# Four attention layers in one kernel: values ahead of background work, and VectorE's softmax chain in memory of its own and in more parts of the final layer

## The chip, the cores and the metric

The kernel runs on one core of a Trainium2 chip. The metric is the device time of one execution in microseconds (us). The engines of the core are TensorE (PE), VectorE (DVE), ScalarE (ACT), GpSimd (POOL) and SyncE (SP, which issues DMAs here). Each works off its own list of instructions in order and waits on semaphores.

## The reference

Four layers act on x of 2048 rows by 640, in bf16, each with 32 heads of 20 columns. Layers 0 and 2 use weights A and a causal window of 256 keys; layers 1 and 3 use weights B and attend to all 2048 keys.

```python
def _A_ref(x, wqkv, wo):          # _B_ref: the same without the mask
    qkv = (x @ wqkv).reshape(B, S, 3, H, Dh).transpose(2, 0, 3, 1, 4)
    q, k, v = qkv[0], qkv[1], qkv[2]
    scores = einsum("bhqd,bhkd->bhqk", q, k) * (Dh ** -0.5)
    mask = (idx[:, None] - idx[None, :] >= 0) & (idx[:, None] - idx[None, :] < 256)
    p = softmax(where(mask, scores, -1e9))
    return einsum("bhqk,bhkd->bhqd", p, v).transpose(0, 2, 1, 3).reshape(B, S, D) @ wo
x = A_x
x = x + _A_ref(_layernorm(x), A_wqkv, A_wo)
x = x + _B_ref(_layernorm(x), B_wqkv, B_wo)
x = x + _A_ref(_layernorm(x), A_wqkv, A_wo)
x = x + _B_ref(_layernorm(x), B_wqkv, B_wo)
```

## The kernel before, in words

**Units, banks and tiles.** The queries are cut into four chunks `c` of 512, the heads into eight groups `g` of four. A *unit* is one layer, chunk and group (`Unit`, L674). A unit's work is a list of *banks*: the scores of 128 keys against 512 queries for one head `j`, which fill one PSUM bank of 128x512 float32. A full unit has 16 key blocks times 4 heads, so 64 banks. The first chunk of layers 1 and 3 is cut into *parts* by key blocks (`PARTS`, L42): layer 1 into four parts of 4 blocks, layer 3 into one of 12 blocks (48 banks) and one of 4. Results of a part that isn't the last are kept in `raw_o`.

**A tile** is what one pass of the main loop (from L1281) handles: three banks, sometimes two or four. PSUM has eight banks: 0 to 2 for the scores of even tiles, 3 to 5 for odd ones (a tile of four takes bank 6 too), 7 for the values' sums (`op`), and bank 6 for everything else. A loop pass, called a tick below, writes instructions in this order:
- the tile's scores on TensorE (L1318), "S" below; if VectorE is to take a bank of it, the first step of that bank's chain follows;
- one exponential on ScalarE over the tile's banks (L1349), into a buffer `pt`;
- `load_ahead`, which issues DMAs of coming units, then `pump` and `keep_clock`: **background work** (projections, layer norm, output products, the tails that divide by the softmax sums), in slices of some 0.2 us of TensorE, by a credit that `rate` (L1258) sets from what is due; `keep_clock` adds matmuls whose results nobody reads (`unread`, L639) where there is too little. All of it goes through bank 6, and each product there must be moved out by VectorE (L323, L568, L1092 and others) before the next may start;
- **the values** (L1382): the probabilities of the tile two or three passes back times v, added up in bank 7; at a unit's end the banks that VectorE computed are multiplied too (L1391), and `finish_unit` (L841) has VectorE copy bank 7 out (L848, L850, L862, L864);
- one step of VectorE's chain (`side_step`, L953), and the masks of windowed tiles on GpSimd and VectorE (L1421, L1431).

The built order of each engine is the order of these calls; nothing reorders it.

**VectorE's chain.** A unit's `aside` (L684) names banks whose exponential VectorE computes, in pairs: two conversions of scores to fixed point (L920, one for each bank), then over both banks L925, L931, L936, L944 and L948. `t_side` (L897) yields after each; a step may be taken when `side["credit"]` is above zero; the credit grows by 0.4 a tick and, once `side_start` (L876) has set `late`, by 1.2 or 1.1. Two kinds of place are used:
- layer 1, chunks 1 to 3: two banks of each unit. Such a bank is the third bank of a tile of two others ("side" in the list made up to L1233), so that the exponential of that tile covers two banks. The chain's three buffers and two outputs lie in `raw_o`, which is free in that time.
- layer 3 from chunk 1 on (after the list, `t >= len(tiles)`): six banks of nearly every unit, whose scores are computed alone into bank 6 (L914). The three buffers are taken from the pool of normalized inputs `xnT` once all of those are free, the outputs from `ka` and `qa`.

The first chunk of layer 3 has no such banks. `xnT` has five buffers (L72), the keys of windowed units 18 (`KA`, L38).

Of the kernel before, what the change touches and what calls it, by code (L numbers as in the profile page):

```python
# [9 lines left out]
BF16 = mybir.dt.bfloat16  # L10
# [27 lines left out]
KA = 18  # L38
SIDE_RATE = 1.2
QA = 4  # L40

# [7 lines left out]
def kernel(  # L49
# [14 lines left out]
    def pool(name, bufs, space=None):  # L64
        kw = {"space": space} if space else {}
        return ctx.enter_context(tc.tile_pool(name=name, bufs=bufs, **kw))
# [4 lines left out]
    vap = pool("vap", 10)  # L71
    xtp = pool("xtp", 5)  # L72
    onp = pool("onp", 2)
# [28 lines left out]
    ka_all = big.tile([P, KA, C], BF16, name="ka", tag="ka")  # L102
    kas = [ka_all[:, n, :] for n in range(KA)]
    qa_all = big.tile([P, QA, C], BF16, name="qa", tag="qa")
# [197 lines left out]
    live = Counter()  # L302
    cap = {"qa": QA, "ka": KA, "va": 10, "xnT": 5, "kt": 3, "vt": 3, "qt": 4, "ln": 1, "w": 4, "vs": 2}

# [369 lines left out]
    class Unit:  # L674
        def __init__(self, l, c, g, part=None):
            self.l, self.c, self.g, self.part = l, c, g, part
            self.windowed = l % 2 == 0
            self.aside = ()
            if self.windowed:
                sets = [(m, b0, subs, j) for m, b0, subs in window_banks(c) for j in range(4)]  # L680
            else:

                if c > 0 and (l, c, g) != (3, 1, 0):
                    self.aside = tuple((NT - 1, j) for j in ((2, 3) if l == 1 else range(4)))  # L684
                    if l == 3 and (c, g) != (NC - 1, G - 1):
                        self.aside += ((NT - 2, 0), (NT - 2, 1))
                k0, k1 = key_blocks(l, part)
                sets = [
                    (None, 0, [(kc, 0, 4, 0)], j) for kc in range(k0, k1) for j in range(4)
                    if (kc, j) not in self.aside  # L690
                ]
            n = len(sets)
            self.banks = [
                (self, j, m, b0, subs, i < 4, i >= n - 4 + len(self.aside), i == n - 1)
                for i, (m, b0, subs, j) in enumerate(sets)
            ]
# [176 lines left out]
    side_out = {}  # L873
    side = {"credit": 0.0, "gen": None, "tiles": None, "late": False}

    def side_start():  # L876

        assert live["xnT"] == 0
        tl = [xtp.tile([P, KD, C], BF16, name="xnT", tag="xnT") for _ in range(3)]
        live["xnT"] += 3  # L880
        f = [v[:, 0:4, :].rearrange("p a b -> p (a b)") for v in tl[0:3]]
        side["tiles"] = [v.bitcast(F32) for v in f]
        side["out"] = deque(ka_all[:, KA - 6 + 2 * n : KA - 4 + 2 * n, :] for n in range(3))
        side["out"].extend(qa_all[:, 2 * n : 2 * n + 2, :] for n in range(2))
        side["late"] = True

    def side_early():

        b = part_o["t"]
        side["tiles"] = [b[:, 2 * n : 2 * n + 2, :].rearrange("p a b -> p (a b)") for n in range(3)]  # L890
        side["out"] = deque(
            b[:, n, :].bitcast(BF16).rearrange("p (a b) -> p a b", a=2) for n in (6, 7)
        )
        side["gen"] = t_side()
        side_step(False)

    def t_side():  # L897

        V = nc.vector
        while aside:  # L900
            u = aside[0]
            for pair in range(len(u.aside) // 2):
                while id(u) not in loaded or (
                    u.l == 3 and (not side["late"] or state["tick"] < loaded[id(u)] + 8)
                ):
                    yield None
                for i in range(2):
                    yield "bank"
                    xi, xm, xw = side["tiles"]
                    if u.l == 3:  # L910
                        mseq[0] += 1
# [17 lines left out]
                yield 0.7  # L929
                power = xw.bitcast(I16)[:, 0 : 2 * C]  # L930
                V.tensor_scalar(  # L931
# [50 lines left out]
    def side_need(u):  # L982

        if u.l == 3:
            n = 0
# [217 lines left out]
    with tc.manual_schedule():  # L1203
# [17 lines left out]
        while n < last_layer:  # L1221
# [4 lines left out]
            if (  # L1226
                len(at) < len(u.aside) and banks[n + 1][0] is u
                and len(tiles) >= 3 * len(at) + (at or [0])[0]
            ):
# [28 lines left out]
        def rate(t):  # L1258
# [11 lines left out]
            return min(1.1 * r, 1.0 if u.l == 0 else 0.9)  # L1270

        last_tick[0] = len(tiles)
        wide_pt = 0
# [7 lines left out]
        while ended is None or t < ended + 8:  # L1281
# [3 lines left out]
            if t < len(tiles) or banks:  # L1285
                if t >= len(tiles) and not side["late"] and not live["xnT"] and not todo:
                    side_start()
# [66 lines left out]
                for i, b in enumerate(cur):  # L1354
                    pts.append((t, pt, i, b))
                state["least"] = (1.76 if state["unit"] >= woven else 1.0) * n_b / 3
                state["floor"] = 0.9 if state["unit"] >= index[1, 1, 0, None] else 0.0
                load_ahead()
                r = rate(t)
                pump(r, r + 0.1)  # L1360
                keep_clock()
            else:
# [3 lines left out]
            for n in range(2 if n_b == 0 or t > closed + 1 else 0):  # L1366
# [30 lines left out]
                if end:  # L1397
# [3 lines left out]
                    break  # L1401

            if n_b:
                side["credit"] = min(side["credit"] + ((SIDE_RATE if state["unit"] < index[3, NC - 1, 0, None] else 1.1) if side["late"] else 0.4), 1.3)
                side_step(False)
# [73 lines left out]
```

## Time and profile before

| | |
|---|---|
| median of 3 runs (lowest to highest) | 2222.56 us (2214.69 to 2223.66) |
| the profiled execution's own time | 2214.42 us |
| its span on the core | 2212.7 us |
| exponentials L1349 on ScalarE | 2104.3 us in 1657 |
| PE, DVE, ACT, POOL busy | 1919.8, 1199.8, 2139.9, 482.5 us |
| two bank counts of L1349: 1536 columns (three banks), 1024 (two) | x1380, x198 |

Where the stages lie in the span, from the starts of L1349 taken tile by tile: layer 0, with the first parts of layer 1 woven in, up to 372 us; the rest of layer 1's first chunk to 492; chunks 1 to 3 of layer 1 with chunks 0 to 2 of layer 2 to 1293.7; the 12-block parts of layer 3 for groups 0 to 3 to 1382.1; chunk 3 of layer 2 to 1424.8; the 12-block parts of groups 4 to 7 to 1512.2; the 4-block parts to 1569.8; chunks 1 to 3 of layer 3 to 2202.0.

Busy times are sums of durations; where one instruction starts before the one ahead of it has ended, durations add up to more than the time that passes, so a price for a stream of them is read from the distance between starts. Idle times in the lines are those just before an instruction, with what ended them.

### The profile page before, as it was taken

The numbers are of one execution on the slowest core, as the hardware profiler recorded it, in microseconds if no ns is written. First come the engines' busy times: TensorE is split into PE (matmuls) and PEld (weight loads), VectorE is DVE, ScalarE is ACT, GpSimd is POOL, SyncE is SP. The second block draws the span as 40 slices with busy tenths as digits, with TensorE's granted clock in tenths as the row PEclk, the third lists the DMA queues.
The fourth block names the chain that finished last, engine by engine and source line by source line (L and its number), as shares of the span: only waits on it lengthen the run. The fifth ranks groups of instructions, "written<-read, shape, count | busy, mean of one in ns | idle before, by whom it ended". The sixth has DMA issues, their size and how long they took to land.

```text
span 2212.7 us, 70085 instructions
## 1 busy us (share of the span) xinstructions
PE 1919.8 (87%) x30415; PEld 756.1 (34%) x30415; DVE 1199.8 (54%) x2190; ACT 2139.9 (97%) x1734; POOL 482.5 (22%) x950
## 2 busy tenths in 40 slices
PE   8889998988888888888888888888888888888888
PEld 4444443333333333333333433342332222222222
DVE  6656564434445454444554533532467767767774
ACT  7889899999999999999999999999999999999998
POOL 6664545200231114301143112511000000000000
PEclk9999999999999999999999999999999999999999
DMA  6233323421211223112230123122121111111100
GB/s 200 74 99 91 88 81 93 102 78 45 74 41 33 71 60 97 33 34 66 66 104 24 48 72 100 36 57 63 54 62 35 32 32 44 32 32 35 49 24 16
DMA packets 88404, 137.09 MB, mean 62 GB/s; under 512 B 20766, under 2 KB 63486, under 8 KB 88094
## 3 DMA queue, kind: packets, MB, share of 16 engines
q1 hardware_dynamic: 68878, 79.43, 13.0%
q0 software_dynamic: 19216, 53.17, 8.1%
q8 instruction: 238, 3.90, 0.7%
q14 instruction: 72, 0.59, 0.1%
HBM read 99.52 MB, written 27.79 MB: 58 GB/s over the span
## 4 chain that ended last, share of the span: by engine, by line
ACT 52%; PE 21%; issue 18%; DVE 6%; DMA 1%; POOL 1%; ACTq 0%; DVEq 0%; POOLq 0%
ACT pt L1349 51%; PE ps L300 12%; PE ps L1318 5%; PE ps L1382 2%; DVE on L1092 1%; DVE st L323 1%; DVE pt L1431 1%; DMA wqk<-in_B_wqkv_dram 1%; PE ps L1088 1%; PE ps L437 0%; DVE on L864 0%; DVE x_sb L568 0%; DVE raw_o L920 0%; POOL pt L1421 0%; DVE xnT L323 0%
## 5 line engine op out<-in xcount | busy, mean ns | idle before, releaser
L1349 ACT ACTIVATE pt<-ps 128x1536 bf16<-128x1536 f32 (+2 forms) x1657 | 2104.3, 1456 | 41.8 <-PE ps L1318 32.1
L1318 PE MATMUL ps<-qt,kt 32*128 32x512 bf16 x3960 | 544.6, 384 | 91.4 <-ACT pt L1349 82.9
L300 PE MATMUL ps<-masks,ident 128*32 128x512 bf16 x5844 | 510.2, 387 | 117.8 <-ACT pt L1349 68.5
L1382 PE MATMUL ps<-pt,vt 128*21 128x512 bf16 x3908 | 397.6, 383 | 1.9 <-issue 1.0
L1318 PEld LDWEIGHTS <-kt 32*128 32x128 bf16 x3960 | 163.4, 91 | 546.4 <-issue 531.0
L300 PEld LDWEIGHTS <-ident 128*32 128x32 bf16 x5844 | 165.3, 94 | 349.9 <-issue 336.7
L1421 POOL TENSOR_SCALAR_AFFINE_SELECT pt<-pt 128x256 bf16<-128x256 bf16 (+2 forms) x505 | 213.8, 445 | 189.0 <-ACT pt L1349 183.5
L300 PE MATMUL ps<-xnT,wqk 128*32 128x512 bf16 x3320 | 224.6, 383 | 15.7 <-DVE st L323 4.0
L323 DVE CAST st<-ps 128x512 bf16<-128x512 f32 x134 | 92.7, 692 | 234.0 <-PE ps L300 230.4
L920 DVE TENSOR_SCALAR xnT<-ps 128x512 int32<-128x512 f32 x136 | 93.6, 688 | 134.1 <-PE ps L914 124.6
L300 PE MATMUL ps<-wop,on 128*32 128x320 bf16 x3712 | 159.8, 301 | 7.1 <-DVE x_sb L568 4.0
L1431 DVE TENSOR_TENSOR pt<-pt,masks 128x512 bf16<-128x512 bf16 (+4 forms) x267 | 112.4, 436 | 96.8 <-ACT pt L1349 94.6
L1382 PEld LDWEIGHTS <-vt 128*21 128x21 bf16 x3912 | 104.8, 91 | 126.1 <-issue 94.1
L300 PEld LDWEIGHTS <-on 128*32 128x32 bf16 x5760 | 113.5, 95 | 74.2 <-issue 51.1
L1318 PE MATMUL ps<-qa,ka 32*128 32x384 bf16 (+2 forms) x1408 | 114.7, 275 | 27.5 <-ACT pt L1349 24.4
L568 DVE TENSOR_TENSOR x_sb<-x_sb,ps 128x320 bf16<-128x320 bf16 x120 | 58.3, 486 | 146.8 <-PE ps L300 146.6
L300 PE MATMUL ps<-wv,xnT 128*32 128x320 bf16 x2560 | 115.2, 301 | 8.3 <-DVE on L1092 2.2
L1092 DVE TENSOR_TENSOR on<-on,ps 128x512 bf16<-128x512 bf16 x128 | 86.3, 684 | 57.9 <-PE ps L1088 56.7
L300 PEld LDWEIGHTS <-wqk 128*32 128x32 bf16 x3320 | 77.1, 95 | 114.4 <-issue 61.9
L864 DVE CAST on<-ps 128x512 bf16<-128x512 f32 x112 | 77.0, 687 | 57.0 <-PE ps L1391 32.6
L536 POOL DMA_DIRECT2D k_d<-st x75 | 43.0, 573 | 233.2 <-DVE st L323 223.2
L404 POOL TENSOR_SCALAR rstd<-mv 128x4 f32<-128x4 f32 x15 | 3.7, 248 | 382.6 <-DVE mv L391 374.4
(100 smaller groups left out, 1537.5 us busy)
## 6 DMA issues: line engine op xcount, KB each, us to landing
vt<-v_d SPq DMA_DIRECT2D x48, 336.0 KB
kt<-k_d SPq DMA_DIRECT2D x192, 80.0 KB
wqk<-in_B_wqkv_dram POOLq DMA_DIRECT2D x80, 160.0 KB, 3.4
wqk<-in_A_wqkv_dram POOLq DMA_DIRECT2D x70, 160.0 KB, 3.6
k_d<-st POOLq DMA_DIRECT2D x75, 128.0 KB, 2.6
q_d<-st POOLq DMA_DIRECT2D x75, 128.0 KB, 2.2
qt<-q_d SPq DMA_DIRECT2D x384, 20.0 KB
v_d<-vs POOLq DMA_DIRECT2D x16, 336.0 KB, 3.0
```

Source lines behind the costliest of these rows:

```text
L300: nc.tensor.matmul(out_[r], lhsT=lhsT[:, r], rhs=rhs, start=start, stop=stop)
L323: nc.vector.tensor_copy(out=out_, in_=in_)
L536: nc.gpsimd.dma_start(out=dst, in_=staging.pop())
L568: nc.vector.tensor_tensor(out=xv, in0=had, in1=yp, op=ALU.add)
L864: nc.vector.tensor_copy(out=oT, in_=op)
L920: V.tensor_scalar(out=xi.bitcast(I32)[:, i * C : (i + 1) * C], in0=side["psum"], scalar1=SCALE * LOG2E * FIX, scalar2=-127.0 * FIX, op0=AL ...
L1092: nc.vector.tensor_tensor(out=oT, in0=oT, in1=zb, op=ALU.mult)
L1318: nc.tensor.matmul(sp[:, i, col * P : (col + qn) * P], lhsT=u.k(kc, j), rhs=u.q(j, q0, qn), start=True, stop=True,)
L1349: nc.scalar.activation(out=pt[:, i:k, b0 * P :], in_=sp[:, i:k, b0 * P :], func=ACT.Exp, scale=SCALE,)
L1382: nc.tensor.matmul(op[32 * j : 32 * j + VW, q0 * P : (q0 + qn) * P], lhsT=u.v(kc, j), rhs=pg[:, i, col * P : (col + qn) * P], start=(first ...
L1421: nc.gpsimd.affine_select(out=v, in_=v, compare_op=ALU.is_gt if later else ALU.is_ge, fill=0.0, base=0, pattern=[[0, k - i], [-1 if later ...
L1431: nc.vector.tensor_tensor(out=pt_[:, i:k, cols], in0=pt_[:, i:k, cols], in1=mv_, op=ALU.mult)
```

## The change

1. Once `state["early"]` is off (from the first part of layer 1 with blocks 12 to 16, tile 307, 434 us), a tick's background work is written after the values instead of ahead of them.
2. The chain gets a tile `side_mem` (10 KB a partition) for its three buffers, and four 512-column blocks of `ka` as two outputs from the start. For this `xnT` goes from five buffers to three, and windowed keys from 18 blocks to 14.
3. Each 12-block part of layer 3's first chunk (eight units) names four banks, those of its last key block, for the chain. They are placed like those of layer 1: third bank of a tile whose exponential covers two, at tiles 0, 3, 8 and 11 of the part (`SIDE_AT`). The credit there grows by 0.9 a tick. (In layer 1 the two banks stay at 0 and 3.)
4. `side_start` no longer waits for `xnT` to be free.

```diff
+SIDE_AT = (0, 3, 8, 11)
-    xtp = pool("xtp", 5)
+    xtp = pool("xtp", 3)
-    kas = [ka_all[:, n, :] for n in range(KA)]
+    kas = [ka_all[:, n, :] for n in range(KA - 4)]
+    side_mem = big.tile([P, 10 * C], BF16, name="side", tag="side")
-    cap = {"qa": QA, "ka": KA, "va": 10, "xnT": 5, ...
+    cap = {"qa": QA, "ka": KA - 4, "va": 10, "xnT": 3, ...
 # Unit.__init__
-                if c > 0 and (l, c, g) != (3, 1, 0):
+                if l == 3 and c == 0 and part[0] == 0:
+                    self.aside = tuple((part[1] - 1, j) for j in range(4))
+                elif c > 0 and (l, c, g) != (3, 1, 0):
 # the chain's memory
-    side = {"credit": 0.0, "gen": None, "tiles": None, "late": False}
+    side = {
+        "credit": 0.0, "gen": None, "late": False,
+        "tiles": [
+            side_mem[:, 0 : 4 * C].bitcast(F32), side_mem[:, 4 * C : 8 * C].bitcast(F32),
+            side_mem[:, 8 * C : 10 * C],
+        ],
+        "out": deque(ka_all[:, KA - 4 + 2 * n : KA - 2 + 2 * n, :] for n in range(2)),
+    }
 # side_start
-        assert live["xnT"] == 0
-        tl = [xtp.tile([P, KD, C], BF16, name="xnT", tag="xnT") for _ in range(3)]
...
-        side["out"] = deque(ka_all[:, KA - 6 + 2 * n : KA - 4 + 2 * n, :] for n in range(3))
+        side["out"].append(ka_all[:, KA - 6 : KA - 4, :])
 # t_side, side_need
-                    u.l == 3 and (not side["late"] or state["tick"] < loaded[id(u)] + 8)
+                    u.l == 3 and u.c and (not side["late"] or state["tick"] < loaded[id(u)] + 8)
-                    if u.l == 3:
+                    if u.l == 3 and u.c:
 # the list of tiles
-                and len(tiles) >= 3 * len(at) + (at or [0])[0]
+                and len(tiles) >= SIDE_AT[len(at)] + (at or [0])[0]
 # main loop
+        def background(t, n_b):
+
+            state["least"] = (1.76 if state["unit"] >= woven else 1.0) * n_b / 3
+            state["floor"] = 0.9 if state["unit"] >= index[1, 1, 0, None] else 0.0
+            r = rate(t)
+            pump(r, r + 0.1)
+            keep_clock()
...
                 load_ahead()
-                r = rate(t)
-                pump(r, r + 0.1)
-                keep_clock()
+                if state["early"]:
+                    background(t, n_b)
...
 # (the values of this tick stand here)
+            if n_b and not state["early"]:
+                background(t, n_b)
             if n_b:
-                ... + ((SIDE_RATE if ... else 1.1) if side["late"] else 0.4), 1.3)
+                ... + ((SIDE_RATE if ... else 1.1) if side["late"] else 0.9 if units[state["unit"]].l == 3 else 0.4), 1.3)
                 side_step(False)
```

More of the change, by code (lines that the diff above doesn't have):

```diff
@@ L302 @@
     live = Counter()
-    cap = {"qa": QA, "ka": KA, "va": 10, "xnT": 5, "kt": 3, "vt": 3, "qt": 4, "ln": 1, "w": 4, "vs": 2}
+    cap = {"qa": QA, "ka": KA - 4, "va": 10, "xnT": 3, "kt": 3, "vt": 3, "qt": 4, "ln": 1, "w": 4, "vs": 2}
     def room(*tags):
@@ L873 @@
     side_out = {}
-    side = {"credit": 0.0, "gen": None, "tiles": None, "late": False}
-    def side_start():
-        assert live["xnT"] == 0
-        tl = [xtp.tile([P, KD, C], BF16, name="xnT", tag="xnT") for _ in range(3)]
-        live["xnT"] += 3
-        f = [v[:, 0:4, :].rearrange("p a b -> p (a b)") for v in tl[0:3]]
-        side["tiles"] = [v.bitcast(F32) for v in f]
-        side["out"] = deque(ka_all[:, KA - 6 + 2 * n : KA - 4 + 2 * n, :] for n in range(3))
+    side = {
[6 more added lines that the diff above has]
+    }
+    def side_start():
+        side["out"].append(ka_all[:, KA - 6 : KA - 4, :])
         side["out"].extend(qa_all[:, 2 * n : 2 * n + 2, :] for n in range(2))
@@ L887, in side_early @@
     def side_early():
[L889 to L893, printed above, removed]
         side["gen"] = t_side()
@@ L929, in t_side @@
                 yield 0.7
-                power = xw.bitcast(I16)[:, 0 : 2 * C]
+                power = xw.bitcast(I16)
                 V.tensor_scalar(
@@ L982, in side_need @@
     def side_need(u):
-        if u.l == 3:
+        if u.l == 3 and u.c:
             n = 0
@@ L1285 @@
             if t < len(tiles) or banks:
-                if t >= len(tiles) and not side["late"] and not live["xnT"] and not todo:
+                if t >= len(tiles) and not side["late"] and not todo:
                     side_start()
@@ L1355 @@
                     pts.append((t, pt, i, b))
-                state["least"] = (1.76 if state["unit"] >= woven else 1.0) * n_b / 3
-                state["floor"] = 0.9 if state["unit"] >= index[1, 1, 0, None] else 0.0
                 load_ahead()
-                r = rate(t)
-                pump(r, r + 0.1)
-                keep_clock()
+                if state["early"]:
+                    background(t, n_b)
             else:
@@ L1401 @@
                     break
+            if n_b and not state["early"]:
+                background(t, n_b)
             if n_b:
-                side["credit"] = min(side["credit"] + ((SIDE_RATE if state["unit"] < index[3, NC - 1, 0, None] else 1.1) if side["late"] else 0.4), 1.3)
+                side["credit"] = min(side["credit"] + ((SIDE_RATE if state["unit"] < index[3, NC - 1, 0, None] else 1.1) if side["late"] else 0.9 if units[state["unit"]].l == 3 else 0.4), 1.3)
                 side_step(False)
```

## The prediction, made before the changed kernel ran

> **What bounds the kernel now.** I read the busy times first, then the costliest groups, then the waits.
>
> ```profile
> PE 1919.8 (87%) x30415; PEld 756.1 (34%) x30415; DVE 1199.8 (54%) x2190; ACT 2139.9 (97%) x1734; POOL 482.5 (22%) x950
> ...
> L1349 ACT ACTIVATE pt<-ps 128x1536 bf16<-128x1536 f32 (+2 forms) x1657 | 2104.3, 1456 | 41.8 <-PE ps L1318 32.1
> ```
>
> ScalarE's exponentials fill the span; 41.8 us of idle stand ahead of them, mostly because the scores (S) came late. So time can be won in two ways: fewer banks for ScalarE, or S on time. The waits say why S comes late: TensorE stands in background work until VectorE has emptied bank 6.
>
> ```profile
> PE ps L300 <- DVE st L323: 22.6, 75, 0.6
> ...
> PE ps L300 <- DVE on L1092: 15.1, 31, 1.7
> ```
>
> (Total, times, longest.) The next view is the timeline, without which neither edit has a price.
>
> ```profile
> 888.96 0.39 PE L1382 MATMUL ps<-pt,va 128*21 128x384 bf16 x8
> ...
> 891.00 0.68 DVE L1092 TENSOR_TENSOR on<-on,ps 128x512 bf16<-128x512 bf16 x1
> ...
> 891.72 0.40 PE L300 MATMUL ps<-masks,ident 128*32 128x512 bf16 x4 [0.85 <-DVE on L1092]
> ...
> 892.38 0.40 PE L1382 MATMUL ps<-pt,vt 128*21 128x512 bf16 x4
> ```
>
> At 890.87 TensorE begins to wait 0.85 us in background work, and the values at 892.38, whose inputs are long there, stand behind it and ahead of the next S. Four column groups run at once: four values products cost the next instruction some 0.22 us.
>
> ScalarE's own pace I take from the distances between starts of L1349: behind a three-bank tile 1.331 us where nothing waits, behind a two-bank tile 0.904 at the least, behind four 1.757. So a bank less is worth up to 0.427 us. The 48 two-bank tiles with a VectorE bank in layer 1 average 1.036, because TensorE's S and background don't fit into 0.904.
>
> VectorE's pace, in a stretch where it has no idle:
>
> ```profile
> 495.62 0.69 DVE L925 TENSOR_SCALAR raw_o<-raw_o 128x1024 f32<-128x1024 uint16 x1
> 496.23 0.69 DVE L931 TENSOR_SCALAR raw_o<-raw_o 128x1024 int16<-128x1024 int16 x1
> 496.83 0.35 DVE L1053 RECIPROCAL rz<-ps 128x32 f32<-128x32 f32 x1
> ```
>
> 0.69 us operations start 0.61 apart. Over all back-to-back pairs the distance is 0.083 below the duration, so I price VectorE by duration less 0.083: conversion 0.61, L925 0.61, L931 0.60, L936 1.14, L944 1.13, L948 0.61. A pair of banks costs 2 x 0.61 + 4.09 = 5.3 us of VectorE.
>
> **The four banks of the 12-block parts.** Here ScalarE is the bound too, and VectorE the idle one:
>
> ```profile
> 1294.00:1382.30 88.30, 77.54 (x1249) 33.01 (x1242) 28.41 (x59) 86.92 (x65) 18.99 (x31) 0.98 0.31 87
> ...
> 1424.80:1512.50 87.70, 75.40 (x1234) 32.62 (x1226) 26.41 (x56) 86.71 (x66) 15.48 (x24) 1.00 0.21 57
> ```
>
> (Window; length; PE, PEld, DVE, ACT, POOL busy; clock; DMA; GB/s.) Two stretches of 64 tiles, 175.8 us from first to last start against a floor of 128 x 1.331 = 170.4, so 5.4 of stalls. In the changed program's order both still have 64 tiles: 48 of three banks, 16 of two. At 0.904 that is 2 x (63.9 + 14.5) = 156.7; at layer 1's 1.036 it is 2 x (63.9 + 16.6) = 161.0. I take 161.0.
>
> VectorE pays: 32 banks are 16 pairs, of which 15.8 fall into these stretches: 83.8 us, beside 25.4 + 23.3 that it has there now (durations less 0.083): 132.5 in 161.0, or 82%. (The busiest 40 us of the last stage, 1825 to 1865, have 32.27 us in 48 operations, so 28.3 and 71%, with 39.29 us of ScalarE busy.) An average below 100% is not enough: a product may enter bank 6 only when VectorE has emptied it, and between two ticks TensorE has about an S and its wait, 0.5 to 1.0 us, as cover. So I laid VectorE's work of each tile, in the changed order, against that tile's pace, carried the rest on, and counted as stall what exceeds a tolerated backlog: 0.5 us gives 4.0 + 2.6, 1.0 gives 1.2 + 0.9. The same count over chunks 1 to 3 of layer 3, before, gives 8.3 at 0.5 where 11.7 of stall were there (1161 to 1620, by tile), so 0.5 is nearest, if a bit low. I take 6.6, and 2 to 3 of today's 5.4, the part that isn't VectorE's (weights landing, TensorE full). 161.0 + 6.6 + 2.4 = 170: **5.8 us won**. Ends: 156.7 with no stall, 19.1 won; with 1.5 times 6.6 and all 5.4 kept, 176.3, 0.5 lost.
>
> Waits added: at a part's end four more values products wait for the chain's last step. Behind them stand bank 7's copy and all of TensorE. In the built order that step comes three tiles ahead, 3.8 us, in all eight parts: nothing, unless the backlog reaches 3 us; then up to one L944, 1.1 us, eight times. The third bank of a two-bank tile holds up S two tiles on until VectorE has read it: that is within the 1.036.
>
> A rule speaks against this. The Trainium skill, SBUF — State Buffer, section "Who interferes with whom", says that a VectorE operation in a two-port mode and GpSimd lock each other out for a whole instruction, the writing of descriptors for GpSimd's DMAs included. The trace doesn't show it: GpSimd's 80 + 70 weight DMAs (L337) take 852 to 977 ns at medians of 867 and 864, though layer 1's chain runs beside many. By the rule each of the some 45 issues in the two stretches could wait up to one wide step, 1.14 us.
>
> By the rows that would not reach the path: weights are asked for four ticks ahead, 5.3 us, and land 3.4 after issue.
>
> **Values ahead.** Nothing is added; up to 434 us the order stays. Behind it the distances of L1349 exceed their floors by 34.7 us in all: 5.2 in the stretches above, 29.5 elsewhere. Of these, 6.3 follow two-bank tiles (TensorE's work, no wait), some 17.8 follow ticks in which background work waited over 0.1 us (59 tiles), the rest ticks without. In the 59, S can come earlier by the values that no longer stand between, at most 0.22 us and at most the stall: 10.0 in sum. But some of those waits also end with S too late by itself, and S already waits for ScalarE in many (0.15 to 0.56 in the timeline). I take 6 of the 10. Ends: 29.5 won (all late S gone); on the other side 3 lost, if copies of bank 7, now ahead of a tick's evacuation, hold bank 6 for 0.61 us at a tenth of the 24 full units of layer 1 and as many of layer 3.
>
> Values could now stand waiting for masks (layers 0 and 2 wait three tiles). From the end of a tile's last mask to the S after which its values would come is 0.7 us at the median over layer 2: no cost; the cover gone, 0.4 for each of 128 tiles at most.
>
> **At nothing.** Memory: the built order loads units as many tiles ahead as before, windowed ones of layer 2 13 to 35; three `xnT` and 14 key blocks suffice. DMA counts of SP and GpSimd are equal. Were a load late, a tile's wait is some 3.4 us. The last stage has 1626 tiles in all instead of 1627, but as 462 x 1.331 + 3 x 1.757 = 620.2 where it was 464 x 1.331 + 1.757 + 0.904 = 620.2. 52 unread products fewer: off the path.
>
> **Sum.** 5.8 + 6 = 12 us, against the profiled 2214.4 (span 2212.7): 2202.4. The median shown, 2222.6, is 8.2 above that execution; from there 2210.5. I forecast between them, 2206.5.
>
> **Rivals.**
> - *The stall eats it.* Bank 6 waits for the chain so often that the parts gain 0 to 3, and values ahead 2 to 4: 5 us, 2213.5. For: 82% of VectorE, in bursts where today only 71% is seen. Against: the stalls of the last stage at that share are 0.03 us a tile.
> - *More than forecast.* No stalls in the parts (13 to 19) and half of the 29.5: 25 us, 2193.5. For: the values fill the very wait that the timeline shows. Against: the two-bank tiles' 1.036.
> - *VectorE becomes the bound: slower.* It is in order, and now and then idles for a TensorE product with chain steps queued behind. It has 132.5 us to do in 175.8; if it can be used to less than 75%, the parts are slower than now. At 65% they take 204, 28 lost, 22 net of values ahead: 2240.5. The 71% seen makes that unlikely, not impossible.
> - *The order does nothing*, since ScalarE's floor hides it: only the 5.8, 2212.5; counted with the first.
>
> **How the numbers follow.** Forecast (9 to 17 won) 0.42, stall eats it or no effect (9 won to 11 lost) 0.36, more 0.12, slower 0.10. By 0.5%, or 11.1 us, which is about what a measurement of this kernel can tell from no change: faster 0.28 of the forecast's 0.42 and the 0.12, so 0.40; same 0.50; slower 0.10. The range leaves out the slower case and half of the larger gain: from 2214.7 less 25, 2190, to the highest run with no gain, 2224.
>
> **What would show it.** Right: L1349 with 31 more of 1024 columns and 34 fewer of 1536; VectorE's busy time in the two stretches up by some 93 us (durations); the stretches near 85 us each; waits of L300 on L323 and L1092 shorter after 434 us outside them. Wrong: the stretches at 88 or more with S waiting behind L300 on VectorE (the backlog), two-bank tiles slower than 1.1 us, or values (L1382) waiting on masks or on L948.

## The result, and the profile after

The changed kernel takes **2225.46 us** (median of 17 runs, 2219.63 to 2234.4); the kernel before, run beside it, 2219.36 (17 runs, 2214.63 to 2224.43). The ratio is 1.0031, interval [1.0022, 1.004]: 0.3% slower, 19 us above the forecast and just above the range's end of 2224. The profiled execution is the slowest of the 17 (2234.4 us, span 2232.7), so its stages are compared with care: 20.0 us of span separate it from the profiled execution of before, 6 to 8 the medians.

The page of the changed kernel; L1358 is the exponential (L1349 before), L1327 its scores S (L1318 before):

```profile
PE 1943.1 (87%) x30363; PEld 748.7 (34%) x30363; DVE 1287.0 (58%) x2302; ACT 2133.3 (96%) x1733; POOL 485.3 (22%) x950
...
L1358 ACT ACTIVATE pt<-ps 128x1536 bf16<-128x1536 f32 (+2 forms) x1654 | 2094.4, 1433 | 65.9 <-PE ps L1327 54.1
```

ScalarE did get less work: 2094.4 us of exponentials instead of 2104.3. But its idle time ahead of them rose from 41.8 to 65.9 us, and nearly all of the rise is "scores late" (32.1 to 54.1). The engine that was relieved now waits for the one that was not.

The windows of the two stretches with the 12-block parts (window, length, PE, PEld, DVE, ACT and POOL busy, granted clock, DMA share, GB/s), to be laid beside those that the prediction shows:

```profile
1300.70:1394.00 93.30, 78.42 (x1229) 30.99 (x1228) 72.48 (x117) 82.64 (x65) 20.09 (x31) 0.98 0.30 81
1436.70:1525.00 88.30, 75.74 (x1206) 30.10 (x1206) 69.32 (x112) 81.34 (x66) 16.30 (x23) 0.98 0.21 57
```

ScalarE's busy time fell by 4.3 and 5.4 us, VectorE's rose from 28.4 and 26.4 to 72.5 and 69.3, and the stretches became longer: 93.3 + 88.3 = 181.6 us where before took 175.8 and the forecast was 170. Behind a two-bank tile the next exponential starts after 1.265 us on average (taken: 1.036; where nothing waits, 0.904, as forecast), behind a three-bank tile after 1.469 (before 1.374).

What TensorE waited for in the first stretch (total us, times, longest). Before:

```profile
PE ps L300 <- DVE st L323: 4.2, 13, 0.5
PE ps L1318 <- ACT pt L1349: 3.8, 10, 0.6
```

After (L302 and L325 are L300 and L323 of before):

```profile
PE ps L302 <- DVE st L325: 7.2, 10, 2.2
PE ps L302 <- DVE x_sb L570: 2.7, 6, 0.8
PE ps L302 <- DVE xnT L325: 1.3, 2, 0.9
...
PE ps L1327 <- ACT pt L1358: 0.9, 2, 0.5
```

Two things are to be read here. Before, S often stood waiting for ScalarE to empty its banks (L1318 <- ACT): that is TensorE's slack, time that a late product may use up for nothing. After, it is nearly gone. And the waits of background work on VectorE are now up to 2.2 us long.

What one such wait does, in the trace's timeline (start, duration, engine, line; in brackets the idle time ahead and what ended it):

```profile
1339.16 0.69 DVE L325 CAST st<-ps 128x512 bf16<-128x512 f32 x1 [0.44 <-PE ps L302]
1339.77 0.69 DVE L926 TENSOR_SCALAR side<-side 128x1024 f32<-128x1024 uint16 x1
1340.38 2.00 DVE L932 TENSOR_SCALAR side<-side 128x1024 int16<-128x1024 int16 x1
1340.69 0.69 POOL L467 MEMSET va<- 128x32 bf16 x4
1340.95 1.83 POOL L339 DMA_DIRECT2D wqk<-in_A_wqkv_dram  x2
...
1342.84 1.22 DVE L937 SCALAR_TENSOR_TENSOR side<-side 128x1024 f32<-128x1024 f32 x1
1343.98 0.68 DVE L325 CAST st<-ps 128x512 bf16<-128x512 f32 x1
1344.71 0.40 PE L302 MATMUL ps<-masks,ident 128*32 128x512 bf16 x4 [2.24 <-DVE st L325]
...
1345.32 0.39 PE L1327 MATMUL ps<-qt,kt 32*128 32x512 bf16 x3
1345.85 1.45 ACT L1358 ACTIVATE pt<-ps 128x1536 bf16<-128x1536 f32 x1 [2.14 <-PE ps L1327]
...
1348.42 1.02 ACT L1358 ACTIVATE pt<-ps 128x1024 bf16<-128x1024 f32 x1 [1.12 <-PE ps L1327]
```

Three steps of the chain stand between two evacuations of bank 6 (L325 at 1339.16 and at 1343.98); two short steps of the layer norm, 0.14 and 0.45 us, lie between them too. The next background product may enter bank 6 only after the second, TensorE waits 2.24 us for it, S comes behind that, and the exponential starts 2.14 us late. This is the longest such wait of the stretch and not a typical one: the ten behind L325 add up to 7.2 us, and 1.3 us of this one is the length of L932, 2.00 us instead of 0.69.

### The profile page after: what moved, and what is told of

The parts are those of the page before. It is cut to its first block, busy times and chain, and to the rows that moved or that the text cites. A ratio compares the mean times of both kernels' runs of the same rounds, so it can differ in the third digit from the quotient of the medians.

```text
span 2232.7 us, 70137 instructions
## 1 busy us (share of the span) xinstructions
PE 1943.1 (87%) x30363; PEld 748.7 (34%) x30363; DVE 1287.0 (58%) x2302; ACT 2133.3 (96%) x1733; POOL 485.3 (22%) x950
## 5 line engine op out<-in xcount | busy, mean ns | idle before, releaser
L1358 ACT ACTIVATE pt<-ps 128x1536 bf16<-128x1536 f32 (+2 forms) x1654 | 2094.4, 1433 | 65.9 <-PE ps L1327 54.1
L1327 PE MATMUL ps<-qt,kt 32*128 32x512 bf16 x3960 | 555.6, 387 | 80.4 <-ACT pt L1358 72.6
L302 PE MATMUL ps<-masks,ident 128*32 128x512 bf16 x5792 | 510.3, 390 | 122.2 <-ACT pt L1358 64.9
L1327 PEld LDWEIGHTS <-kt 32*128 32x128 bf16 x3960 | 163.4, 91 | 489.8 <-issue 475.2
L302 PEld LDWEIGHTS <-ident 128*32 128x32 bf16 x5792 | 175.7, 94 | 301.0 <-issue 273.9
L921 DVE TENSOR_SCALAR side<-ps 128x512 int32<-128x512 f32 x216 | 148.6, 688 | 165.3 <-PE ps L915 122.3
L302 PE MATMUL ps<-xnT,wqk 128*32 128x512 bf16 x3320 | 225.0, 384 | 16.5 <-DVE rT L1072 4.5
L325 DVE CAST st<-ps 128x512 bf16<-128x512 f32 x134 | 92.6, 691 | 181.5 <-PE ps L302 181.1
L1388 PEld LDWEIGHTS <-vt 128*21 128x21 bf16 x3880 | 97.8, 89 | 259.3 <-issue 255.6
L302 PE MATMUL ps<-wop,on 128*32 128x320 bf16 x3712 | 159.7, 301 | 9.6 <-DVE x_sb L570 7.2
L302 PEld LDWEIGHTS <-on 128*32 128x32 bf16 x5760 | 119.8, 96 | 69.7 <-issue 35.7
L1327 PE MATMUL ps<-qa,ka 32*128 32x384 bf16 (+2 forms) x1408 | 116.6, 278 | 22.4 <-ACT pt L1358 19.4
L937 DVE SCALAR_TENSOR_TENSOR side<-side 128x1024 f32<-128x1024 f32 x108 | 132.1, 1223 | 3.0
L302 PE MATMUL ps<-wv,xnT 128*32 128x320 bf16 x2560 | 115.7, 302 | 9.6 <-DVE on L1093 3.8
L302 PEld LDWEIGHTS <-wqk 128*32 128x32 bf16 x3320 | 83.9, 96 | 99.7 <-issue 42.8
L945 DVE SCALAR_TENSOR_TENSOR ka<-side 128x1024 bf16<-128x1024 f32 x82 | 99.6, 1214 | 0.6
```

Source lines behind the costliest of these rows:

```text
L302: nc.tensor.matmul(out_[r], lhsT=lhsT[:, r], rhs=rhs, start=start, stop=stop)
L325: nc.vector.tensor_copy(out=out_, in_=in_)
L921: V.tensor_scalar(out=xi.bitcast(I32)[:, i * C : (i + 1) * C], in0=side["psum"], scalar1=SCALE * LOG2E * FIX, scalar2=-127.0 * FIX, op0=AL ...
L937: V.scalar_tensor_tensor(out=xi, in0=xm, scalar=EA, in1=xm, op0=ALU.add, op1=ALU.mult)
L945: V.scalar_tensor_tensor(out=po, in0=xi, scalar=EB, in1=xm, op0=ALU.add, op1=ALU.mult)
L1327: nc.tensor.matmul(sp[:, i, col * P : (col + qn) * P], lhsT=u.k(kc, j), rhs=u.q(j, q0, qn), start=True, stop=True,)
```

## The experiments

All ratios are to the kernel before, run beside on the same chip; over 123 runs it has a median of 2217.1 us. "Parts" means the two stretches together, from first to last start, in the kernel's one profiled execution; between executions with the same parts they differ by a few us (180.6 to 184.5 for the four kernels with four banks and the full chain as the change has them).

### Which part of the change costs the time

**e1: the order alone.** The kernel before with background work behind the values from 434 us on.

```diff
-                r = rate(t)
-                pump(r, r + 0.1)
-                keep_clock()
+                if state["early"]:
+                    background(t, n_b)
...
+            if n_b and not state["early"]:
+                background(t, n_b)
```

> The kernel before with one edit: background work after the values from tile 307 on; memory and banks as before. Theory 1 (VectorE's queue in the 12-block parts costs the time, the order is worth something): 3 to 6 us faster than before, 12-block parts at 175 us (first to last start, both stretches), and the waits of background work on VectorE shorter. Theory 2 (the new order costs): 3 to 8 us slower than before, with the parts near 176. Theory 3 (TensorE's half-clock stretches cost, whatever starts them): the time follows the granted clock, some 1.3 us for each 0.001 of it, and this run's clock lies below that of the kernel before if the order is what starts them.

Measured: 2217.75 us, ratio 0.9992 [0.9982, 1.0002]; parts 173.3. That is 1.8 us won, 4 at the interval's end, not 6; the interval includes no change.

**e2: the four banks alone.** The changed kernel with the old order (background ahead of the values throughout).

```diff
-                if state["early"]:
-                    background(t, n_b)
+                background(t, n_b)
...
-            if n_b and not state["early"]:
-                background(t, n_b)
```

> The changed kernel with the background work put back ahead of the values; new memory and the four banks of the 12-block parts stay. Theory 1: slower than before by 8 to 12 us, since the parts keep their loss of 6 us or more and the values stand behind the waits again (parts 182 to 187 us). Theory 2: 0 to 5 us faster than before, parts near 172. Theory 3: the time lies where the clock puts it.

Measured: 2223.87 us, 1.003 [1.0016, 1.0044]; parts 180.6. The whole loss is there without the new order. It is a little less than forecast (8 to 12 us, parts 182 to 187).

**e3: the memory alone.** The kernel before with `side_mem`, three `xnT` and 14 key blocks, no new banks, old order.

```diff
-    xtp = pool("xtp", 5)
+    xtp = pool("xtp", 3)
...
+    side_mem = big.tile([P, 10 * C], BF16, name="side", tag="side")
```

> The changed kernel without its new order and without the banks of the 12-block parts: only the chain's own memory, three xnT and 14 key blocks are left of the change. All theories: within 2 us of before, 48 distances behind two-bank tiles of layer 1 at 1.03 on average. If memory matters after all (a buffer that comes free too late), over 3 us slower, with waits on DMA or on xnT.

Measured: 2218.44 us, 1.0003 [0.9992, 1.0015]; parts 174.9. The memory costs nothing that these runs can tell, as forecast.

### Why the parts became longer

**e4: four banks with a short chain.** In the 12-block parts the chain ends after the conversions and one step (L921, L921, then L932's operation straight into the output). Left out of the computation: the correction of the exponential's fraction (L926, L937, L945, L949) in these 32 banks.

```diff
+                if u.l == 3 and u.c == 0:
...
+                    pt = side["out"].popleft()
+                    V.tensor_scalar(
+                        out=pt.rearrange("p a b -> p (a b)").bitcast(I16),
+                        in0=xi.bitcast(I16)[:, 1::2],
+                        scalar1=127.0, scalar2=128.0, op0=ALU.add, op1=ALU.mult,
+                    )
+                    side_out.setdefault(id(u), []).append(pt)
+                    yield 0.7
+                    continue
```

> The changed kernel, but in the 12-block parts a pair of banks takes only its two conversions and one 0.6 us step: L926, L937, L945 and L949 are left out there (the exponential of those 32 banks is then only its power of two, so part of the computation is left out). VectorE's work for a pair falls from 5.3 to 1.8 us, everything on ScalarE and TensorE stays. Theory 1: the parts fall from 181.5 to 161 to 165 us and the kernel is 12 to 18 us faster than the changed one. A rival to it (TensorE can't keep a two-bank tile's pace, whatever VectorE does): the parts stay over 175 us. Theory 3: the parts fall only as far as half-clock stretches in them go, 5 us at the most.

Measured: 2213.35 us, 0.9978 [0.9965, 0.999]; parts 168.8. Its windows, columns as above:

```profile
1295.60:1381.50 85.90, 77.49 (x1232) 30.70 (x1229) 44.94 (x84) 81.92 (x66) 19.07 (x31) 1.00 0.33 89
1424.20:1507.10 82.90, 74.64 (x1206) 30.11 (x1206) 41.81 (x80) 80.41 (x65) 15.77 (x23) 1.00 0.23 61
```

ScalarE's busy time is within 1 us of the changed kernel's; only VectorE has 55 us less. So VectorE's chain accounts for 181.6 - 168.8 = 12.8 us of the parts, a little of it perhaps through the clock: counting what each distance between starts exceeds its floor (1.331 or 0.904), the changed kernel has 24.9 us, 2.7 of them at half clock, and e4 has 12.1, all at full clock. Those 12.1 are also what e4 stays above ScalarE's floor of 156.7; the forecast was 161 to 165.

**e5: two banks instead of four**, in the new order.

```diff
-                    self.aside = tuple((part[1] - 1, j) for j in range(4))
+                    self.aside = tuple((part[1] - 1, j) for j in range(2, 4))
```

> The changed kernel with two banks of each 12-block part for VectorE instead of four (one pair, at tiles 0 and 3). VectorE's load in the parts falls from 132 to some 90 us, ScalarE's floor rises from 156.7 to 163.5. If VectorE's queue costs the time: parts (first to last start, both stretches) at 171 to 175 against 181.5 with four and 175.8 with none, and the kernel 6 to 10 us faster than the changed one. If the two-bank tiles as such cost it (TensorE): half of the loss stays, parts near 178 to 179.

Measured: 2213.81 us, 0.9987 [0.9978, 0.9995]; parts 172.2.

```profile
1295.73:1382.86 87.13, 77.78 (x1237) 30.48 (x1233) 50.01 (x88) 84.69 (x65) 19.56 (x31) 1.00 0.32 87
1425.68:1510.75 85.07, 75.63 (x1214) 30.11 (x1210) 47.62 (x84) 83.66 (x66) 15.11 (x23) 1.00 0.22 59
```

With half the added load VectorE is busy 57% of the stretches instead of 78%. The parts are 1.1 us below e1's 173.3, which single profiles can't tell from no gain: with no banks and the new order they are 173.2 to 175.1 (e1, e10, e13, e17), with two banks 172.2, 172.2 and 174.7 (e5, e11, e14). The other 16 banks take them to 181.6, 9.4 longer. Both pairs relieve ScalarE alike. The second pair lies at other tiles (8 and 11); no run has it alone, but e4 has both pairs at these places and is 12.8 us shorter, so the places by themselves don't cost it.

**e6 and e8: smaller steps, or fewer in a row.** e6 cuts L937 and L945 into halves of 512 columns in the parts; e8 lets at most one step of the chain be taken in a tick there.

```diff
+                halves = ((0, C), (C, 2 * C)) if u.l == 3 and u.c == 0 else ((0, 2 * C),)
+                for a, b in halves:
+                    V.scalar_tensor_tensor(
+                        out=xi[:, a:b], in0=xm[:, a:b], scalar=EA, in1=xm[:, a:b],
+                        op0=ALU.add, op1=ALU.mult,
+                    )
+                    yield 1.2 / len(halves)
```

```diff
-            if bank:
+            if bank or units[state["unit"]].part == PARTS[3][0] and units[state["unit"]].l == 3:
```

> The changed kernel; in the 12-block parts each of the two wide chain steps (1.14 us) is cut into two halves of some 0.6 us, which take a credit each, so that a move out of bank 6 stands behind a shorter step; VectorE's total grows by some 2 us. If it is the length of the single step in front of the move that costs: parts at 172 to 177. If it is the queue as a whole or TensorE: 181 to 185, the kernel 0 to 3 us slower than the changed one.

> The changed kernel; in the 12-block parts the chain takes one step a tick and never two, with the same steps and the same total. If bursts cost (two chain steps and a move in one tick): parts at 174 to 178, the kernel 3 to 7 us faster than the changed one. If the total of VectorE's queue or TensorE costs: within 2 us of the changed kernel, parts 180 to 183.

Measured: e6 2224.25 us, 1.0035 [1.0021, 1.0049], parts 180.2; e8 2227.89 us, 1.0044 [1.003, 1.0057], parts 178.6. Halving the steps changes nothing clear of the spread, so the length of a single step is not the cause. e8 lies between its two forecasts in the parts and its kernel is not faster. Nor does it take away the bursts that it was to take away: in its trace two or more chain steps follow each other without a pause at 32 places of the parts, three or more at 9, against 22 and 14 in the changed kernel. So the sum of the chain is what is left as the cause, and how much of it acts through bursts stays open.

### Why the order won so little

My first reading of e1: with the values ahead, `finish_unit` too stands ahead of background in its tick, so a tail's first step, due two ticks later (`yield ("wait", 2)` in `t_tail`), runs one step earlier in the engines' order than before. e13 lets it wait three ticks, in the new order.

```diff
-        yield ("wait", 2)
+        yield ("wait", 2 if state["early"] or final else 3)
```

> Order alone (as in e1_order_only), but the division by the softmax sums (t_tail) starts one tick later, where it stood before the change: with background work behind finish_unit it had moved a tick forward. If the earlier tails are why the new order gained so little (waits of background work on L1092 went from 8.6 us in 20 to 16.2 in 40 behind 434 us): those waits back at 8 to 10 us, all waits of background work on VectorE at 40 instead of 50, and 2 to 4 us faster than order alone. If the waits only follow from VectorE's queue: the sum stays near 50 us and the time within 1 us of order alone.

Measured: 2211.41 us, 0.9968 [0.9956, 0.998]. The same line was then put into the kernel before (e15, old order) and into the changed kernel (e16), and made four ticks in e13's kernel (e17).

```diff
-        yield ("wait", 2 if state["early"] or final else 3)
+        yield ("wait", 2 if state["early"] or final else 4)
```

> The kernel before, old order, with the tails' first wait at three ticks instead of two behind 434 us. If the order's missing gain was the tail's first step running a tick too early relative to the copy of bank 7 (my theory), the delay does nothing in the old order, where that copy stood behind background already: ratio 0.999 to 1.001. If the later tail is a gain by itself, whatever the order (rival), 0.997 like the order with the later tail, and then the order as such is worth nothing.

> The changed kernel, all parts, with the tails' first wait at three ticks instead of two behind 434 us. If the order with the later tail is worth its 5 to 6 us beside the four banks as well, 2219 to 2221, ratio 1.000 to 1.001, that is 5 us below the changed kernel's 1.0031 to 1.0044. If the four banks leave no room for it (the parts are paced by VectorE and TensorE in any order), 1.003 to 1.004 as before.

> Values ahead alone, with the tails' first wait at four ticks instead of three. If three ticks are what the copy of bank 7 needs and no more, the same 0.997 within the interval, the waits on the tail's products (15.2 us in 38 at three ticks) unchanged. If the tail still meets its copy at three, the waits go below 12 us and the ratio to 0.995 or 0.996.

Measured: e15 2218.75 us, 1.0005 [0.9992, 1.0017]; e16 2219.38, 1.0011 [0.9999, 1.0023]; e17 2212.41, 0.9979 [0.9969, 0.999]. So the later tail is worth nothing in the old order and 0.0024 (e13) or 0.0013 (e17) in the new one, against e1: the two belong together, and with both the order wins 0.2 to 0.3%, 5 to 7 us. Beside the four banks it takes 0.0020 off, and leaves them at no gain. Three ticks are enough: a fourth wins nothing more.

What the waits of TensorE say behind 434 us, e1 first, then e13 (L1092 is a tail's product, L323 and L568 other evacuations of bank 6):

```profile
PE ps L300 <- DVE on L1092: 16.2, 40, 0.9
PE ps L300 <- DVE st L323: 11.3, 25, 0.8
PE ps L300 <- DVE x_sb L568: 8.6, 28, 0.7
PE ps L300 <- DVE rT L1071: 4.0, 6, 1.5
```

```profile
PE ps L300 <- DVE on L1092: 15.2, 38, 0.8
PE ps L300 <- DVE st L323: 11.4, 28, 0.5
PE ps L300 <- DVE x_sb L568: 7.3, 25, 0.7
```

Before, in the same window:

```profile
PE ps L300 <- DVE st L323: 22.6, 75, 0.6
PE ps L300 <- DVE on L1092: 8.6, 20, 0.8
```

The order did halve the waits on L323; 7.6 of those 11.3 us came back on L1092. All waits of background work on VectorE add up to 48.2 us before, 50.0 in e1, 43.4 in e13, 48.4 in e17; 59.6 in e15; 67.3 in the changed kernel, 58.3 in e16. The sums go the right way in e13 and e16, but L1092 itself, which I had named, hardly falls (16.2, 15.2, 14.4 at two, three, four ticks). And e15 has 11.4 us more of these waits than before in the same time, so their sum is not a price. That the pair of edits works is measured; by which of the waits is not, and my first reading, the tail that runs too early, is not shown.

### The clock, and the products that nobody reads

**e7: no unread products in the 12-block parts**, since TensorE seemed full there; **e9: more of them** from tile 1118 on (1525 us).

```diff
+            if units[state["unit"]].l == 3 and units[state["unit"]].part == PARTS[3][0]:
+                state["least"] = state["floor"] = 0.0
```

```diff
-            state["least"] = (1.76 if state["unit"] >= woven else 1.0) * n_b / 3
+            state["least"] = (2.1 if t >= 1118 else 1.76 if state["unit"] >= woven else 1.0) * n_b / 3
```

> The changed kernel; in the 12-block parts keep_clock adds no unread products (12 groups fewer in the first stretch, 29 in the second, 0.22 us of TensorE each, so 9 us). If TensorE is the bound there, with every wait on VectorE added to 78 and 76 us of its own work: parts 172 to 175 and the kernel 6 to 9 us faster than the changed one, unless its clock falls. If VectorE is the bound whatever TensorE does: parts 179 to 182. If the half-clock stretches come from too little work: more of them in and behind the parts, and the gain is lost.

> The changed kernel with more unread products behind the 12-block parts (keep_clock's aim 2.1 a three-bank tile instead of 1.76 from tile 1118 on). If TensorE falls to half clock there because it has too little to do: fewer half-clock stretches behind 1525 us (20.7 us of them in the changed kernel's profile), mean clock up by 0.002 to 0.004, and 2 to 5 us faster than the changed kernel. If those stretches come from elsewhere: the same clock, and 0 to 3 us slower, for the added work.

Measured: e7 2225.47 us, 1.0038 [1.0026, 1.005], parts 180.5; e9 2226.16, 1.0036 [1.0023, 1.0049]. Neither makes the kernel faster. e7's windows:

```profile
1298.00:1390.60 92.60, 77.31 (x1157) 32.12 (x1157) 71.91 (x114) 81.66 (x66) 18.14 (x29) 0.91 0.30 80
1433.00:1521.00 88.00, 74.48 (x1072) 29.76 (x1070) 69.11 (x111) 81.27 (x65) 15.76 (x23) 0.86 0.19 50
```

The 8% fewer matmuls (2229 for 2435) take no less time, and the granted clock fell to 0.91 and 0.86: TensorE spent 41 us of the two stretches at half its clock. That length, 180.5, is also what "VectorE is the bound whatever TensorE does" had forecast (179 to 182), but the trace speaks against it: TensorE's waits other than ahead of S fell from 24.9 us to 7.8, those ahead of S rose from 2.5 to 21.0 (ScalarE's banks again), and of the stalls of L1358 (L1360 here) those at full clock fell from 22.2 to 13.9 us, while those at half clock rose from 2.7 to 9.9. What the parts would take without the lost clock, no run shows.

So the unread products are themselves a part of the waits, which I had overlooked. They go through bank 6 like the rest: in the changed kernel's parts 6.3 us of the 24.9, in 11 waits, are TensorE waiting for VectorE to empty bank 6 for a product that nobody reads, with nothing behind it but the next S.

In e9 the profile shows 3.4 us of half clock in the last stage where the changed kernel's had 20.7, the mean clock of its runs is 0.9923 instead of 0.9903, as forecast, and yet the time is the same; that the added products cost in TensorE what they buy in clock fits this, and is not shown apart.

### Where VectorE does have room

**e10** drops the four banks and gives VectorE a pair in every second 4-block part instead (new order); **e11** has this and e5's two banks; **e12** is e5 in the old order; **e14** is e11 with e13's tail.

```diff
+                elif l == 3 and c == 0 and g % 2 == 0 and part[0] > 0:
+                    self.aside = ((NT - 1, 2), (NT - 1, 3))
...
-                and len(tiles) >= SIDE_AT[len(at)] + (at or [0])[0]
+                and len(tiles) >= (SIDE_AT if u.part != PARTS[3][1] else (0, 1))[len(at)] + (at or [0])[0]
```

> The new order and memory; no banks for VectorE in the 12-block parts, but one pair in every second 4-block part of layer 3 (8 banks, at tiles 0 and 1 of the part). There VectorE has 12.8 us of work in 57.6, and 56 of TensorE's groups are unread products. If a bank is won where both VectorE and TensorE have room: that stage falls from 57.6 to 54.5 to 56, the kernel 3 to 6 us faster than before. If a two-bank tile doesn't pay anywhere: the stage stays at 57 or over.

> Two banks in each 12-block part, as in the run with two, and the pairs in the 4-block parts. If both add: 12-block parts at 172, 4-block stage at 54.5 to 56, the kernel 5 to 8 us faster than before. If the clock takes it back: spans as said for the stages but mean clock 0.002 lower than before's, and 2 to 4 us faster.

> Two banks in each 12-block part with the background work ahead of the values, as before the change. If the new order is worth what order alone showed (some 2 us): 1 to 3 us slower than the run with two banks and the new order, so near the kernel before. If the two banks do it: within 1 us of that run.

> Two banks in each 12-block part, a pair in every second 4-block part, new order, and the tails a tick later. If the tails cost: 2 to 4 us faster than the same without the delay (ratio to the kernel before 0.9965 or lower). If not: 0.997 to 0.9985.

Measured: e10 2214.73 us, 0.9986 [0.9974, 0.9999]; e11 2212.83, 0.9978 [0.9965, 0.999]; e12 2215.09, 0.9996 [0.9981, 1.001]; **e14 2210.8, 0.9968 [0.9955, 0.998]**, the fastest median. The 4-block stage takes 56.4 us in e10 and 56.0 in e11, 57.6 before and 57.9 in the changed kernel: four pairs gain about 1.5. e5 and e12 differ by 0.0009, within their intervals, so with two banks the order's worth is not told. (e12's parts are 178.6 us, 6 more than e5's, but in an execution 10.8 us above its kernel's median, with one stall of 4.3 us.) e14's ratio is no better than e13's, so most of what beats the kernel before is the order with the later tail, not more work for VectorE.

## Why the prediction was wrong

**The four banks: the step that failed** is "161.0 + 6.6 + 2.4 = 170"; measured 181.6. The counts in it held: ScalarE's work fell by 4.3 + 5.4 us in the windows, VectorE's load (durations less 0.083) is 132.9 us where I had 132.5. What failed is what I set against them, and all three terms were too small. With the chain cut short (e4), a two-bank tile takes 1.124 us where I took layer 1's 1.036, which is 2.8 us over 32 tiles, and three-bank tiles keep 5.0 us of stalls where I took 2.4; the backlog then costs 12.8 where I took 6.6. Together that is the miss of 11.6. In the two stretches every moment of TensorE is either its own work or a wait, so the length can be split (idle time ahead of its instructions, from the trace):

| | parts | TensorE's own | waits ahead of S | all other waits |
|---|---|---|---|---|
| before | 175.8 | 152.8 | 11.8 | 11.2 |
| e1, order alone | 173.3 | 152.1 | 13.2 | 8.0 |
| e5, two banks | 172.2 | 153.5 | 5.5 | 13.2 |
| e4, four banks, short chain | 168.8 | 152.3 | 5.2 | 11.3 |
| changed kernel | 181.6 | 154.1 | 2.5 | 24.9 |

TensorE's own work is 152 to 154 us whatever the banks, and some 11 us of other waits were there before. These make 152 + 11 = 163, and e4 shows that with a light chain the parts stop at 168.8, not at ScalarE's 156.7. I took layer 1's 1.036 us as a price for TensorE's fullness, but never added up TensorE itself for this stage: its 77.54 + 75.40 us of 176 stood in the lines I showed, 87% of the stretch then and 98% of the 156.7 that I set as the end. So that end was out of reach. The 163 is no more than the 161.0 + 2.4 = 163.4 of my sum, though; the 5.4 us by which e4 exceeds it are about the 5.2 that TensorE still waits ahead of S. As I read it, it is early at some tiles and late at others, and being early doesn't pay for being late; a sum over the stretch can't see that. (VectorE still has 77.1 us of load in e4, so a part of the 5.4 may be its own; no run takes that away.)

The larger term is the backlog of VectorE: 24.9 - 11.3 = 13.6 us of waits more than e4, less the 2.7 that it takes from the waits ahead of S, and 1.8 more of own work: 12.8 net with rounding, where I had 6.6. The count I made (work of each tile against a tolerated backlog of 0.5 us) was calibrated on chunks 1 to 3, where a wait of background work is partly paid by S's slack. Here 6.6 of the 11.8 us of that slack are gone even with the short chain (5.2 left); that the same backlog cost about twice as much for this reason is argued, not shown. The end of my range for this term, 1.5 times 6.6 with all 5.4 kept (176.3), was too near by 5.

Two of the signs named in advance for "wrong" appeared: stretches of 88 or more (93.3 and 88.3) with TensorE behind L302 on VectorE, and two-bank tiles above 1.1 us (1.265).

**The rivals.** "VectorE becomes the bound" is the one that came true in kind: it named the sign, the place (chain steps ahead of evacuations in one in-order queue), and the point, 75% usable. VectorE's 132.9 of 181.6 us are 73%. Its price was oversized: I worked it at 65%, 28 us; 5.8 were lost. I gave it 0.10 because 71% had been seen in the last stage; there bank 6 is shared in the same way, but the scores are not pressed by two-bank tiles, which may be the difference; no run tests it. By its number the result, 6 to 8 us lost, lies in the band of "the stall eats it or no effect" (9 won to 11 lost, 0.36), but that rival had the parts gain 0 to 3.

**Values ahead: 6 won was wrong for the edit as it stands; it is reached with the tail a tick later, which the sum did not contain, so that match is luck.** e1 gives 1.8 us (0.9992 of 2217). The step "I take 6 of the 10" kept the waits of background work as they were and only took the values out from behind them; but `finish_unit` moved with the values and the tails with it, and 7.6 of the 11.3 us of waits lost on L323 came back on L1092. e13 has 7 us, e17 5, e15 nothing. As the waits on L1092 stay in e13, why the later tail pays is open.

**At nothing:** memory held (e3). The last stage's 620.2 = 620.2 was right by tiles; in the profiled execution it is 5.4 us longer, with 17.3 us more at half clock, but e10 and e11, with the changed kernel's tiles there, take 632.3 and 631.4 us where before has 632.2: so not the tiles.

**The rule weighed against the trace** was dismissed too lightly. The Trainium skill, SBUF — State Buffer, section "Who interferes with whom", says that VectorE in a two-port mode and GpSimd shut each other out for a whole instruction. In the timeline above, L932 takes 2.00 us at 1340.38 instead of its 0.69, just while GpSimd runs L467 and L339. That agrees with the rule, though no run here takes GpSimd's work away and the trace doesn't tell the mode of L932, so the cause is argued. I had looked at GpSimd's durations and priced GpSimd's wait for a wide step of 1.14 us, though that step (L936) reads two tensors and the section names copies, casts and tensor_scalar for such modes; the victim was VectorE, in a tensor_scalar of 0.69 us. L932 took 0.97 to 1.02 us instead of 0.69 at six other places of the changed kernel, each beside an L339 that had begun before it; in before L931 took 0.97 at three, so the trace did show it. So it is a few us of VectorE in all, about 1.3 at the one place where it reached the path.

**What is left: the clock.** Within the runs of one kernel, the time falls by 1.3 us for each 0.001 of the granted clock's mean (123 runs of before; the changed kernel 1.4 in 17). The mean clock of the changed kernel's runs is 0.9903, that of before 0.9937, which goes with some 4.5 us of the 7.8 between their mean times; at equal clock about 3 are left. In e16 it is 0.9933, in e13 and e17 0.9955 and 0.9958. But e14 and e15, with the later tail too, have 0.9938, so the tail alone does not steady it. That part of what the waits cost is paid through the clock is likely, and not shown. Why the stages outside the parts lost clock in the changed kernel is open: of the 20 us between the two profiled executions 5.2 arise before 434 us, where the order is the same, 5.8 in the parts and 5.4 in the last stage, and that first stretch has from 3.4 to 24 us of half clock in single profiles of the kernels here.

## What to carry to other kernels

When work is moved from a full engine to an idle one, add up the third engine as well: here TensorE's own time and its old waits (152 + 11 us) made a floor that stood above the relieved engine's 156.7, and as the slack ahead of the scores went (11.8 us, then 2.5), the waits on VectorE went into the time. Ask of each wait what it is for: a part of these stood ahead of products that nobody reads. Half the shift (two banks, VectorE at 57%) cost nothing in the new order and brought little; the second half cost 9.4 us of the parts. And when calls change places, follow every call that moves with them: the tails' delay of two ticks had been set for the old order, and one tick more turned the new order from 0.9992 into 0.9968 (0.9979 with two ticks more).

## What the runs showed of the hardware

**A stall of some 2 us can be followed by a window at half clock.** The three windows of 3.41 us around the stall in the changed kernel's timeline above; the number ahead of the DMA share is the granted clock:

```profile
1339.62:1343.03 3.41, 2.57 (x34) 0.84 (x34) 3.37 (x6) 3.41 (x3) 2.97 (x8) 1.00 0.82 176
1343.03:1346.45 3.42, 1.00 (x27) 0.59 (x27) 3.42 (x5) 1.28 (x2) 0.00 (x0) 1.00 0.55 147
1346.45:1349.86 3.41, 3.26 (x58) 1.72 (x57) 2.60 (x7) 1.87 (x2) 0.00 (x0) 0.50 0.02 5
```

In the second window TensorE is busy for 1.00 of 3.42 us; in the third its clock is 0.50, and the next exponential, at 1348.42, in that window, is late by another 1.12 us. Only a part of that is the clock's: its S takes 0.61 us there instead of 0.39, but a wait of 0.88 us on VectorE stands ahead of it too. Half-clock stretches inside these traces are 3.41 us long or a multiple of it, and ahead of them TensorE was busy for 0.27 to 0.83 of a window; a window with 0.47 (before, at 1269.6) was followed by full clock, so no bound follows from one window's busy time. The Trainium skill, TensorE: Matmul & The Clock Gate, section "🔬 Part 1: The HAM clock gate (the "warmup" mystery)", describes such a gate with free-running windows of about 3.4 us; the lengths here agree.

**Once low, the clock can stay low though TensorE is busy.** In e7, whose parts have no unread products:

```profile
1432.58:1435.99 3.41, 2.55 (x41) 1.06 (x39) 3.03 (x6) 3.41 (x4) 3.15 (x6) 1.00 0.07 12
1435.99:1439.41 3.42, 3.02 (x49) 0.90 (x48) 2.40 (x5) 3.42 (x4) 0.00 (x0) 0.50 0.31 91
1439.41:1442.82 3.41, 3.22 (x23) 0.67 (x19) 3.31 (x7) 3.41 (x4) 0.00 (x0) 0.50 0.00 0
1442.82:1446.23 3.41, 2.90 (x29) 1.07 (x30) 2.27 (x4) 3.38 (x4) 0.00 (x0) 0.50 0.00 0
1446.23:1449.65 3.42, 3.42 (x43) 1.28 (x38) 0.57 (x2) 1.66 (x2) 0.00 (x0) 0.50 0.00 0
1449.65:1453.06 3.41, 3.41 (x69) 1.69 (x69) 3.38 (x5) 3.15 (x3) 0.00 (x0) 1.00 0.03 7
```

Here 2.55 busy of 3.41 us were followed by four windows at half clock, through 3.02, 3.22 and 2.90 of busy time; full clock came back only behind a window that was full to 3.42. ScalarE's busy time is 3.4 us in three of the four, so these cost little by themselves. It is one place, and where the two bounds lie is not known from it.
